# Linear attention and two expert layers on one core: 1 KB runs for the first half block of k, and zero products of a constant

## The chip, the core and the metric

One core of a Trainium2 chip runs the whole program. The metric is device time in microseconds (us): 813.32 us before the change, the median of 3 runs (813.06 to 813.55).

## What is computed

Three layers follow each other, all in float32, on 4 batches of 576 tokens with 8 heads of 64.

```python
q_p, k_p = (phi(q_s), phi(k_s))                # phi: exp(h - max(h)), h = x @ omega.T - |x|^2 / 2
kv = np.einsum('bhsm,bhsd->bhmd', k_p, v)
z = np.sum(k_p, axis=2)
num = np.einsum('bhsm,bhmd->bhsd', q_p, kv)
den = np.einsum('bhsm,bhm->bhs', q_p, z)[..., None] + 1e-06
...
h = x @ w_in
g = np.maximum(h, 0.0) + np.log1p(np.exp(-np.abs(h)))
x = g @ w_out
...
a, b = x @ w1, x @ w2
return ((a * b) @ w3) @ w_out
```

The term |x|^2 / 2 is the same for all features of a token, and so falls out with the maximum that is subtracted.

## The kernel before

The work goes through the k stage (features of k, and their sums with v), the q stage (features of q, the attention's output and its transposes), and then the two expert layers, which are long rows of products. Most products are made three times with operands split into a high and a low part (float32r); the first ones are made in plain f32.

The k stage has eight half blocks i of 512 tokens for four heads each (two half blocks to a batch; the remaining 64 tokens of each batch lie in krest). Half block i is four pieces t of 128 tokens. `load_k(i)` (lines 300 to 307) loads it into one of four buffers rawk. For i > 0 that is one DMA; half block 0 comes as four DMAs, one a piece, so that work can start on the first: pieces 0 and 2 on SyncE's queue (SP), pieces 1 and 3 on ScalarE's (ACT), behind omega (`om`). In DRAM a partition's row of a half block is two pairs of heads with 512 tokens each, so a piece is two runs of 512 B a partition.

`split_k(i)` (lines 309 to 314) makes the high part kt*h on VectorE (DVE) and the low part kt*l. Half block 0 isn't split, but multiplied in f32 (`om`, `rawk`, 8 products in 16 passes). Half block 1 is split in four pieces, the low part on GpSimd (POOL), the others in one piece, the low part on VectorE. `k_feat(i, t)` (lines 362 to 367) multiplies a piece with omega (`project`), takes the maximum of each head on VectorE (`nmax`, line 349), and has ScalarE take the exponentials (`kp`, line 354, four of 128x128 a piece). `kv_sum(i)` multiplies them with v (`vt`) and with the rest (`vrest`, `kpr`), half an array at a time.

TensorE (PE) makes three zero products at the very start, before any data is there. They read a small tile, `edge_t`, that GpSimd has to set to zero first:

```python
warm = ps()
for _ in range(WARM):
    matmul(warm[:, 0:256], edge_t[:, 0:1].to_broadcast([128, 128]), edge_t[:, 0:1].to_broadcast([128, 256]), True, True)
```

The queues are in order: an engine's instructions wait for each other, and so do SyncE's DMAs. The order on each engine is not the order of the code. A scheduler lays it out when the program is built, by its own estimates of durations, so an edit in one place can move instructions elsewhere. The preparation of the first weights (`Job`, lines 138 to 191: `ends` on ScalarE, `upper`, `lower`, the sums and the low parts on VectorE) is mixed into the k and q stages in this way, and so are the casts of q (`qt`).

Of the kernel before, what the change touches and what calls it, by code (L numbers as in the profile page):

```python
# [19 lines left out]
F32 = mybir.dt.float32  # L20
FR = mybir.dt.float32r
# [6 lines left out]
B, H, S, D = 4, 8, 576, 64  # L28
# [4 lines left out]
KT = 4  # L33
# [12 lines left out]
KBUF = 3  # L46
# [13 lines left out]
FOLD_RATE = 2.2  # L60
LAST_RATE = 1.2
KEEP = 4
WARM = 3
WO_AHEAD = 3
GAP = 3
FILL = [18, 19, 20]
# [5 lines left out]
def body(ctx: ExitStack, tc: tile.TileContext, q, k, k_rest, v, v_rest, om_t, w_in, w_out, w12, w3, wo, out):  # L72
    nc = tc.nc
# [9 lines left out]
    def ps():  # L83
        return ps_.tile([128, 512], F32, tag="ps", name="ps")
# [10 lines left out]
    def matmul(o, a, b, start, stop, **kw):  # L95
        nc.tensor.matmul(out=o, lhsT=a, rhs=b, start=start, stop=stop, **kw)  # L96

    def mm3(o, ahi, alo, bhi, blo, first, last, **kw):
        matmul(o, ahi, bhi, first, False, **kw)
        matmul(o, ahi, blo, False, False, **kw)  # L100
        matmul(o, alo, bhi, False, last, **kw)

    ident = cp.tile([128, 128], F32, name="ident")
# [161 lines left out]
    edge_t = edge.tile([128, 24], F32, name="edge")  # L265
# [3 lines left out]
    K_ = kstack.enter_context(tc.tile_pool(name="K_", bufs=1, side="right"))  # L269
# [4 lines left out]
    def pair(name, bufs):  # L274
        n = small.get(name, (None, 1))[1]
        if n:
            small[name] = sm.tile([128, 2, 4], F32, tag=name, bufs=bufs, name=name), 0
        else:
            small[name] = small[name][0], 1
        return small[name][0][:, 1 - bool(n)]  # L280
# [9 lines left out]
    kt, vt, kps, kpr, kvs, qts, kacc, raw = {}, {}, {}, {}, {}, {}, {}, {}  # L290
# [5 lines left out]
    def split(hi, lo, f, low=None):  # L296
        nc.vector.tensor_copy(out=hi, in_=f)
        (low or nc.gpsimd).tensor_tensor(out=lo, in0=f, in1=hi.bitcast(F32), op=ALU.subtract)

    def load_k(i):  # L300
        if i < 2 * B:
            raw[i] = K_.tile([128, 2, 512], F32, tag="rawk", bufs=4, name="rawk")
            if i:
                nc.sync.dma_start(out=raw[i], in_=k[i])
            else:
                for t in range(KT):
                    (nc.scalar if t % 2 else nc.sync).dma_start(out=raw[i][:, :, 128 * t:128 * t + 128], in_=k[i][:, :, 128 * t:128 * t + 128])

    def split_k(i):
        if 0 < i < 2 * B:  # L310
            kt[i] = kt[i - KBUF] if i > KBUF else [K_.tile([128, 2, 512], FR, name=f"kt{i}{x}") for x in "hl"]
            n = 128 if i == 1 else 512
            for o in range(0, 512, n):
                split(*[x[:, :, o:o + n] for x in (*kt[i], raw[i])], nc.gpsimd if i == 1 else nc.vector)

    def load_v(i):
        if i < 2 * B:
# [21 lines left out]
    def project(lhs):  # L339
        pj = ps()  # L340
        for p in range(2):
            a = lhs(p)
            if len(a) == 2:
                mm3(pj[:, 256 * p:256 * p + 256], *a, *om_s, True, True)
            else:
                matmul(pj[:, 256 * p:256 * p + 256], *a, om, True, True)
        pj = pj.rearrange("p (h m) -> p h m", h=4)
        nmax = pair("nmax", 4)
        nc.vector.tensor_reduce(out=nmax, in_=pj, axis=AX.X, op=ALU.max, negate=True)  # L349
        return pj, nmax  # L350

    def features(pj, nmax, dst):
        for h in range(4):
            nc.scalar.activation(out=dst[:, h, :], in_=pj[:, h, :], func=AF.Exp, bias=nmax[:, h:h + 1])  # L354
# [3 lines left out]
    def flush(n):  # L358
        while len(waiting) > n:
            waiting.pop(0)()  # L360

    def k_feat(i, t):
        if t == 0:
            kps[i] = K_.tile([128, KT, 4, M], F32, tag="kp", bufs=3, name="kp")
        p = project(lambda p: [x[:, p, 128 * t:128 * t + 128] for x in kt.get(i, [raw[0]])])
        waiting.append(lambda: features(*p, kps[i][:, t]))
        flush(0)

# [325 lines left out]

    nc.scalar.dma_start(out=om, in_=om_t)
    load_k(0)
    nc.scalar.preload_act_table_set("exp_and_others")
    warm = ps()
    for _ in range(WARM):
        matmul(warm[:, 0:256], edge_t[:, 0:1].to_broadcast([128, 128]), edge_t[:, 0:1].to_broadcast([128, 256]), True, True)  # L700
    make_identity(nc, ident)
    nc.vector.tensor_scalar(out=om, in0=om, scalar1=float(D) ** -0.25, scalar2=None, op0=ALU.mult)
    split(*om_s, om)
# [9 lines left out]

    load_krest(0)
    load_k(1)
    split_k(1)
    load_v(0)
    load_vrest(0)
    load_k(2)
    split_k(2)  # L720
    load_v(1)
    load_k(3)
# [76 lines left out]
    for s in range(NW):  # L799
        n = min(WB, NF * 512 - WB * s)  # L800
# [351 lines left out]
def _layout(i):  # L1152
    import numpy as np

    def words(a):
        return np.ascontiguousarray(a).view(np.int64)

    q = i["q"].transpose(1, 3, 0, 2).reshape(4, 128, NT // 128, 128).transpose(2, 1, 0, 3)
    k = i["k"].transpose(0, 1, 3, 2).reshape(B, 2, 2, 128, S)
    k_main = k[..., :512].reshape(2 * B, 2, 128, 512).transpose(0, 2, 1, 3)  # L1160
    k_rest = k[..., 512:].reshape(B // 2, 2, 2, 2, 128, 64).transpose(4, 0, 2, 3, 1, 5).reshape(128, B, 2, 128)
    v = np.ones((B, 2, S, 4, D + 1), i["v"].dtype)
    v[..., :D] = i["v"].reshape(B, 2, 4, S, D).transpose(0, 1, 3, 2, 4)
    v_main = v[:, :, :512].reshape(2 * B, KT, 128, 4, D + 1).transpose(0, 2, 1, 3, 4)
    v_rest = v[:, :, 512:].reshape(B // 2, 2, 2, 64, 4, D + 1).transpose(1, 3, 0, 2, 4, 5).reshape(128, B, 4, D + 1)

    om = np.zeros((128, 2 * M), i["omega"].dtype)
    om[:D, :M] = om[D:, M:] = i["omega"].T

    def rows(w, n):  # L1170
        return w.reshape(-1, n, 128, w.shape[1]).transpose(0, 2, 1, 3).reshape(-1, 128, n * w.shape[1])

    def blocks(w, n):
        r, c = w.shape
        return w.reshape(r // 128, 128, c // 128 // n, n, 128).transpose(2, 1, 3, 0, 4).reshape(c // 128 // n, 128, -1)

    def quads(w):

        x = w.reshape(2, 2, 128, -1, 2, 128).transpose(3, 2, 0, 4, 1, 5)
        x = np.stack([x[:, :, 0, 0], x[:, :, 0, 1], x[:, :, 1, 1], x[:, :, 1, 0]], axis=2)  # L1180
        return x.reshape(x.shape[0], 128, 1024)

    w12 = np.stack([i["moe2_w1"].reshape(DM, NJ, 128), i["moe2_w2"].reshape(DM, NJ, 128)], axis=2).reshape(DM, -1)
    return {
        "q": np.ascontiguousarray(q),
        "k": np.ascontiguousarray(k_main),
        "k_rest": np.ascontiguousarray(k_rest),
        "v": np.ascontiguousarray(v_main),
        "v_rest": np.ascontiguousarray(v_rest),
        "om": om,  # L1190
        "w_in": words(quads(i["moe_w_in"])),
        "w_out": words(rows(i["moe_w_out"], NF)[0]),
        "w12": words(quads(w12)),
        "w3": words(blocks(np.ascontiguousarray(i["moe2_w3"].T), 1)),
        "wo": words(rows(i["moe2_w_out"], 1)),
    }
# [19 lines left out]
```

## Time and profile before

| what | value |
|---|---|
| median of 3 runs | 813.32 us (813.06 to 813.55) |
| the profiled execution's own time | 814.26 us |
| its span, first to last instruction | 812.1 us |
| TensorE busy (PE), 5462 products | 805.6 us, 99% |
| weight loads busy (PEld) | 752.9 us, 93% |
| VectorE busy (DVE) | 599.9 us, 74% |
| ScalarE busy (ACT) | 442.0 us, 54% |
| GpSimd busy (POOL) | 25.8 us, 3% |
| moved by DMA | 150.04 MB, 185 GB/s in the mean |

Shares are means over stages with different limits; a stage is to be read by itself. A product's record begins when it enters the array and its end is modelled, so products overlap in the records, and their spacing tells the pace. An f32 product stands as two records. A row of a timeline gives the start in us, the time that the merged records cover, the engine, the line, what is written from what, and in brackets how long the engine was idle before, and what ended that.

### The profile page before, as it was taken

The page shows a single profiled execution, that of the slowest core. Times are in us where ns is not written, and L with a number is a line of the kernel's source. Part 1 is how long each engine was busy: PE and PEld are TensorE (multiplying, and loading weights), DVE is VectorE, ACT ScalarE, POOL GpSimd, SP SyncE. Part 2 cuts the span into 40 slices and gives each one's busy share as a digit, 9 for nine tenths or more (in the row PEclk, how much of TensorE's full clock was granted, in tenths as well). Part 3 has the DMA queues.
Part 4 walks back from the last instruction along what each step waited for, and adds up shares of the span by engine and source line. Part 5 has one row for each costly group of instructions (what it writes and reads, how often), then busy time and mean ns, then how long its engine had stood idle before and what let it go on. Part 6 is the DMA issues. An engine that isn't in the chain of part 4 may idle for free.

```text
span 812.1 us, 14425 instructions
## 1 busy us (share of the span) xinstructions
PE 805.6 (99%) x5462; PEld 752.9 (93%) x5462; DVE 599.9 (74%) x1019; ACT 442.0 (54%) x862; POOL 25.8 (3%) x29
## 2 busy tenths in 40 slices
PE   9999999999999999999999999999999999999998
PEld 8989999999999998888888889999999998889998
DVE  6899899878755676755469733898988776889951
ACT  6899998557445676745456522422434223674430
POOL 3033300000000000000000000000000000000000
PEclk9999999999999999999999999999999999999999
DMA  9833535665545558687994632365565556353212
GB/s 279 339 97 107 175 98 165 208 207 216 198 148 195 184 191 264 209 262 293 320 308 149 221 117 76 147 217 182 172 217 210 188 176 235 116 171 130 78 49 79
DMA packets 75861, 150.04 MB, mean 185 GB/s; under 512 B 7184, under 2 KB 44688, under 8 KB 75792
## 3 DMA queue, kind: packets, MB, share of 16 engines
q1 hardware_dynamic: 64016, 101.55, 37.6%
q10 hardware_dynamic: 11776, 47.57, 17.3%
q8 instruction: 43, 0.70, 0.4%
q14 instruction: 26, 0.21, 0.1%
HBM read 98.24 MB, written 50.86 MB: 184 GB/s over the span
## 4 chain that ended last, share of the span: by engine, by line
PE 92%; ACT 4%; DVE 3%; DMA 1%; issue 1%; POOL 0%; DVEq 0%; ACTq 0%; POOLq 0%
PE ps L96 89%; PE ps L409 2%; ACT kp L354 2%; PE ps L439 1%; DMA xq<-xd 1%; ACT qp L354 1%; DVE s L462 0%; DVE c L517 0%; DVE nmax L349 0%; ACT f L138 0%; ACT raw L139 0%; DVE u L517 0%; DVE f L142 0%; DVE f L148 0%; ACT kv L389 0%
## 5 line engine op out<-in xcount | busy, mean ns | idle before, releaser
L96 PE MATMUL ps<-dhi,lo 128*128 128x512 f32 x256 | 99.6, 389 | 0.0
L96 PE MATMUL ps<-dlo,hi 128*128 128x512 f32 x256 | 99.6, 389 | 0.0
L96 PE MATMUL ps<-dhi,hi 128*128 128x512 f32 x256 | 99.4, 389 | 0.0
L517 DVE TENSOR_TENSOR c<-ps,u 128x384 f32<-128x384 f32 x144 | 71.5, 549 | 0.9
L642 DVE TENSOR_TENSOR dlo<-dn,dhi 128x512 fp32r<-128x512 f32 x64 | 43.8, 689 | 38.3 <-ACT dhi L641 23.7
L517 DVE TENSOR_TENSOR u<-ps,p 128x384 f32<-128x384 f32 x48 | 26.7, 556 | 56.3 <-PE ps L96 54.6
L138 ACT ACTIVATE f<-raw,bias 128x1024 f32<-128x1024 int16 (+2 forms) x43 | 46.5, 1089 | 35.6 <-DMA raw<-in_w 9.7
L641 ACT CAST dhi<-dn 128x512 fp32r<-128x512 f32 x64 | 39.3, 617 | 44.6 <-DVE dlo L642 26.6
L142 DVE SCALAR_TENSOR_TENSOR f<-raw,f 128x1024 int32<-128x1024 f32 (+2 forms) x43 | 45.1, 1049 | 23.3 <-ACT raw L139 22.7
L557 ACT ACTIVATE c<-c 128x384 f32<-128x384 f32 x72 | 35.0, 524 | 45.7 <-DVE c L517 42.2
L524 ACT COPY p<-ps 128x384 f32<-128x384 f32 x48 | 23.0, 480 | 63.3 <-PE ps L96 45.9
L96 PEld LDWEIGHTS ps<-dhi,lo 128*128 128x128 f32 x256 | 48.0, 188 | 10.1
L96 PEld LDWEIGHTS ps<-dlo,hi 128*128 128x128 f32 x256 | 48.0, 188 | 10.0
L96 PEld LDWEIGHTS ps<-dhi,hi 128*128 128x128 f32 x256 | 48.0, 188 | 9.8
L349 DVE TENSOR_REDUCE nmax<-ps 128x4 f32<-128x512 f32 x72 | 46.6, 682 | 6.1 <-PE ps L96 5.4
L139 ACT ACTIVATE raw<-raw,bias 128x1024 f32<-128x1024 int16 (+2 forms) x43 | 46.4, 1083 | 0.5
L148 DVE SCALAR_TENSOR_TENSOR f<-raw,f 128x1024 int32<-128x1024 int32 (+2 forms) x43 | 45.0, 1046 | 0.5
L354 ACT ACTIVATE qp<-ps,nmax 128x128 f32<-128x128 f32 x144 | 44.3, 542 | 1.1 <-DVE nmax L349 1.1
L354 ACT ACTIVATE kp<-ps,nmax 128x128 f32<-128x128 f32 x128 | 35.6, 485 | 7.4 <-DVE nmax L349 7.2
L96 PE MATMUL ps<-xs1h,thi 128*128 128x384 f32 x96 | 32.3, 336 | 0.2 <-DVE c L517 0.2
L96 PE MATMUL ps<-xs2h,thi 128*128 128x384 f32 x96 | 32.3, 336 | 0.0
L96 PE MATMUL ps<-xs2l,thi 128*128 128x384 f32 x96 | 32.3, 336 | 0.0
(257 smaller groups left out, 2342.3 us busy)
## 6 DMA issues: line engine op xcount, KB each, us to landing
dn<-gd SPq DMA_DIRECT2D x64, 256.0 KB, 4.2
raw<-in_w ACTq DMA_DIRECT2D x16, 1023.8 KB, 5.8
gd<-c SPq DMA_DIRECT2D x80, 192.0 KB, 3.5
pd<-c SPq DMA_DIRECT2D x48, 192.0 KB, 2.3
raw<-in_w_out ACTq DMA_DIRECT2D x10, 767.8 KB, 4.8
raw<-in_w_in ACTq DMA_DIRECT2D x6, 1023.8 KB, 5.2
rawq<-in_q SPq DMA_DIRECT2D x18, 256.0 KB, 2.9
xd<-xs SPq DMA_DIRECT2D x18, 256.0 KB, 2.9
```

The lines of the kernel that those rows point to most:

```text
L96: nc.tensor.matmul(out=o, lhsT=a, rhs=b, start=start, stop=stop, **kw)
L138: nc.scalar.activation(out=self.f, in_=top, func=AF.Relu, scale=TOP, bias=bias[:, 0:1])
L139: nc.scalar.activation(out=self.words(1, F32, 2), in_=top, func=AF.Identity, scale=TOP, bias=bias[:, 1:2])
L142: nc.vector.scalar_tensor_tensor(out=self.f.bitcast(I32), in0=self.words(1, F32, 2), scalar=-2.0 ** 31, in1=self.f, op0=ALU.max, op1=ALU.min)
L148: nc.vector.scalar_tensor_tensor(out=fi, in0=self.words(0, I32, 2), scalar=13, in1=fi, op0=ALU.logical_shift_right, op1=ALU.bitwise_or,)
L349: nc.vector.tensor_reduce(out=nmax, in_=pj, axis=AX.X, op=ALU.max, negate=True)
L354: nc.scalar.activation(out=dst[:, h, :], in_=pj[:, h, :], func=AF.Exp, bias=nmax[:, h:h + 1])
L517: nc.vector.tensor_tensor(out=z, in0=bank, in1=y, op=ALU.add)
L524: nc.scalar.copy(out=p6, in_=b1)
L557: nc.scalar.activation(out=dst, in_=src, func=AF.Softplus)
L641: nc.scalar.copy(out=hi, in_=got[m])
L642: nc.vector.tensor_tensor(out=lo, in0=got.pop(m), in1=hi.bitcast(F32), op=ALU.subtract)
```

## The change

The zero products become five of 128 columns instead of three of 256, and they read a column of zeros that the framework sets up itself, ahead of the barrier at which the engines start. The layout of k puts the four pieces of a half block one behind the other, so that a piece is one run of 1 KB a partition; the tiles rawk and kt* follow it. Piece 3 of half block 0 moves from ScalarE's queue to SyncE's.

```diff
-WARM = 3
+WARM = 5
...
-            raw[i] = K_.tile([128, 2, 512], F32, tag="rawk", bufs=4, name="rawk")
+            raw[i] = K_.tile([128, KT, 2, 128], F32, tag="rawk", bufs=4, name="rawk")
...
-                    (nc.scalar if t % 2 else nc.sync).dma_start(out=raw[i][:, :, 128 * t:128 * t + 128], in_=k[i][:, :, 128 * t:128 * t + 128])
+                    (nc.scalar if t == 1 else nc.sync).dma_start(out=raw[i][:, t], in_=k[i][:, t])
...
-            kt[i] = kt[i - KBUF] if i > KBUF else [K_.tile([128, 2, 512], FR, name=f"kt{i}{x}") for x in "hl"]
-            n = 128 if i == 1 else 512
-            for o in range(0, 512, n):
-                split(*[x[:, :, o:o + n] for x in (*kt[i], raw[i])], nc.gpsimd if i == 1 else nc.vector)
+            kt[i] = kt[i - KBUF] if i > KBUF else [K_.tile([128, KT, 2, 128], FR, name=f"kt{i}{x}") for x in "hl"]
+            n = 1 if i == 1 else KT
+            for t in range(0, KT, n):
+                split(*[x[:, t:t + n] for x in (*kt[i], raw[i])], nc.gpsimd if i == 1 else nc.vector)
...
-        p = project(lambda p: [x[:, p, 128 * t:128 * t + 128] for x in kt.get(i, [raw[0]])])
+        p = project(lambda p: [x[:, t, p, :] for x in kt.get(i, [raw[0]])])
...
+    zeros = nc.const_aps.tensor_like(0.0, ident)
     for _ in range(WARM):
-        matmul(warm[:, 0:256], edge_t[:, 0:1].to_broadcast([128, 128]), edge_t[:, 0:1].to_broadcast([128, 256]), True, True)
+        matmul(warm[:, 0:128], zeros, zeros, True, True)
...
-    k_main = k[..., :512].reshape(2 * B, 2, 128, 512).transpose(0, 2, 1, 3)
+    k_main = k[..., :512].reshape(2 * B, 2, 128, KT, 128).transpose(0, 2, 3, 1, 4)
```

With the tiles, the order of the instructions changes in the k stage and the first half of the q stage; behind that each engine has the same order as before. Three places of it follow.

The start of SyncE's queue, before and then changed (rawk from in_k at L307 are pieces of half block 0, at L304 whole half blocks):

```order
L307 DMA rawk<-in_k 128x2x128 x2
L708 DMA krest<-in_k_rest 128x512
L304 DMA rawk<-in_k 128x1024
L319 DMA vt<-in_v 128x1040
L712 DMA vrest<-in_v_rest 64x1040
```

```order
L307 DMA rawk<-in_k 128x256 x3
L709 DMA krest<-in_k_rest 128x512
L304 DMA rawk<-in_k 128x1024
L319 DMA vt<-in_v 128x1040
L713 DMA vrest<-in_v_rest 64x1040
```

Three pieces stand ahead of everything else instead of two.

VectorE from the second piece of half block 0 on, before and then changed (kt1, kt2 and kt3 are the buffers of half blocks 1, 2 and 3, h and l the high and low parts; nmax is the maximum of one piece):

```order
L349 TENSOR_REDUCE nmax<-ps 128x4 x2
L297 CAST kt1h<-rawk 128x2x128 x4
L349 TENSOR_REDUCE nmax<-ps 128x4 x5
L297 CAST kt2h<-rawk 128x1024
L349 TENSOR_REDUCE nmax<-ps 128x4
L298 TENSOR_TENSOR kt2l<-rawk,kt2h 128x1024
L349 TENSOR_REDUCE nmax<-ps 128x4 x2
L297 CAST kt3h<-rawk 128x1024
```

```order
L349 TENSOR_REDUCE nmax<-ps 128x4 x2
L297 CAST kt1h<-rawk 128x256 x4
L349 TENSOR_REDUCE nmax<-ps 128x4 x6
L297 CAST kt2h<-rawk 128x1024
L349 TENSOR_REDUCE nmax<-ps 128x4
L298 TENSOR_TENSOR kt2l<-rawk,kt2h 128x1024
L349 TENSOR_REDUCE nmax<-ps 128x4
L297 CAST kt3h<-rawk 128x1024
```

One reduction has moved from behind the split of half block 2 to the place ahead of it.

VectorE when the buffers kt1 to kt3 are filled for the second time, half blocks 4 to 6, before and then changed:

```order
L297 CAST kt1h<-rawk 128x1024
L298 TENSOR_TENSOR kt1l<-rawk,kt1h 128x1024
L297 CAST kt2h<-rawk 128x1024
L349 TENSOR_REDUCE nmax<-ps 128x4
L298 TENSOR_TENSOR kt2l<-rawk,kt2h 128x1024
L349 TENSOR_REDUCE nmax<-ps 128x4 x3
L297 CAST kt3h<-rawk 128x1024
L298 TENSOR_TENSOR kt3l<-rawk,kt3h 128x1024
L349 TENSOR_REDUCE nmax<-ps 128x4 x4
```

```order
L297 CAST kt1h<-rawk 128x1024
L298 TENSOR_TENSOR kt1l<-rawk,kt1h 128x1024
L349 TENSOR_REDUCE nmax<-ps 128x4
L297 CAST kt2h<-rawk 128x1024
L349 TENSOR_REDUCE nmax<-ps 128x4
L298 TENSOR_TENSOR kt2l<-rawk,kt2h 128x1024
L349 TENSOR_REDUCE nmax<-ps 128x4 x2
L297 CAST kt3h<-rawk 128x1024
L349 TENSOR_REDUCE nmax<-ps 128x4
L298 TENSOR_TENSOR kt3l<-rawk,kt3h 128x1024
```

One reduction stands ahead of the cast of kt2h that stood behind it, and one more between the two steps of kt3.

## Rows read from the trace of the kernel before

**Rows 1.** Busy by stretch: PE, PEld, DVE, ACT, POOL (count); clock, DMA share, GB/s.

```profile
10.00:60.00 50.00, 48.80 (x851) 45.65 (x850) 46.02 (x66) 46.58 (x160) 9.39 (x9) 1.00 0.71 244
60.00:125.00 65.00, 64.39 (x892) 59.87 (x891) 59.46 (x158) 63.49 (x187) 12.87 (x10) 1.00 0.41 123
125.00:812.00 687.00, 683.35 (x3695) 640.39 (x3693) 490.98 (x788) 328.36 (x509) 0.00 (x0) 1.00 0.55 186
```

**Rows 2.** Timeline of TensorE's products and weight loads in the first 4 us.

```profile
0.92 2.93 PE L96 MATMUL ps<-edge 128*128 128x256 f32 x6 [0.92 <-POOL edge L266]
3.64 0.63 PE L96 MATMUL ps<-om,rawk 128*128 128x256 f32 x1
...
0.91 2.21 PEld L96 LDWEIGHTS ps<-edge 128*128 128x128 f32 x6 [0.91 <-POOL edge L266]
```

**Rows 3.** Timeline of the other engines and of the DMA issues, first 3.5 us.

```profile
0.24 0.10 POOL L1204 MEMSET const-float32-0.0<- 128x1 f32 x1 [0.24 <-issue]
...
0.81 0.09 DVE L259 MEMSET bias<- 128x1 f32 x2 [0.81 <-PEq L1204]
2.84 0.29 DVE L702 TENSOR_SCALAR om<-om 128x256 f32<-128x256 f32 x1 [1.94 <-DMA om<-in_om]
...
0.75 1.32 SPq L307 DMA_DIRECT2D rawk<-in_k  x2
...
0.74 0.39 ACTq L695 DMA_DIRECT2D om<-in_om  x1
```

**Rows 4.** DMA issues from 0.7 to 1 us: KB each, us from issue to landing.

```profile
om<-in_om ACTq DMA_DIRECT2D x1, 128.0 KB, 2.1
rawk<-in_k SPq DMA_DIRECT2D x1, 128.0 KB, 2.6
```

**Rows 5.** DMA queues: q10 (ACT) in 1.7:2.2, q1 (SP) in 2.5:2.75; packets, MB, share.

```profile
q10 hardware_dynamic: 85, 0.08, 48.5%
...
q1 hardware_dynamic: 141, 0.07, 93.4%
```

**Rows 6.** Timeline of TensorE from 4 to 8 us, products and weight loads.

```profile
4.06 1.49 PE L96 MATMUL ps<-om,rawk 128*128 128x256 f32 x3
6.17 0.81 PE L96 MATMUL ps<-om,rawk 128*128 128x256 f32 x3
...
5.57 2.52 PEld L96 LDWEIGHTS ps<-om,rawk 128*128 128x128 f32 x12 [0.74 <-DMA rawk<-in_k]
```

**Rows 7.** Timeline of VectorE from 8 to 16 us, and the product that uses kt2l first.

```profile
8.58 1.99 DVE L297 CAST kt1h<-rawk 128x256 fp32r<-128x256 f32 x4 [1.08 <-DMA rawk<-in_k]
10.49 3.07 DVE L349 TENSOR_REDUCE nmax<-ps 128x4 f32<-128x512 f32 x5
14.68 1.21 DVE L298 TENSOR_TENSOR kt2l<-rawk,kt2h 128x1024 fp32r<-128x1024 f32 x1
...
16.05 0.28 PE L96 MATMUL ps<-omh,kt2l 128*128 128x256 f32 x1
```

**Rows 8.** Timeline of VectorE and of ScalarE from 24 to 31 us.

```profile
24.34 0.69 DVE L297 CAST kt2h<-rawk 128x1024 fp32r<-128x1024 f32 x1
24.94 0.68 DVE L349 TENSOR_REDUCE nmax<-ps 128x4 f32<-128x512 f32 x1
...
25.66 1.14 ACT L354 ACTIVATE kp<-ps,nmax 128x128 f32<-128x128 f32 x4 [1.40 <-DVE nmax L349]
27.39 3.21 ACT L354 ACTIVATE kp<-ps,nmax 128x128 f32<-128x128 f32 x12 [0.59 <-DVE nmax L349]
31.05 1.14 ACT L354 ACTIVATE kp<-ps,nmax 128x128 f32<-128x128 f32 x4 [0.17 <-DVE nmax L349]
```

**Rows 9.** Timeline of TensorE from 48 to 63 us, where it waited for ScalarE.

```profile
49.89 0.34 PE L96 MATMUL ps<-vt,kp 128*64 128x65 f32 x4 [0.44 <-ACT kp L354]
...
58.19 1.88 PE L409 MATMUL ps<-ident,qp 128*128 128x128 f32 x7 [0.28 <-ACT qp L354]
...
62.29 0.84 PE L409 MATMUL ps<-ident,qp 128*128 128x128 f32 x3 [0.36 <-ACT qp L354]
```

## The prediction

> **What bounds the kernel now.** I read the busy times by stretch first. TensorE is busy for 48.8 of the 50 us from 10 to 60, 64.4 of 65 from there to 125, and 683.4 of 687 after that; ScalarE (the fourth pair) has 46.6 of 50 and 63.5 of 65 in the first two and 328 of 687 in the last [rows 1]. So after 125 us only TensorE counts, and the change leaves the order of the instructions there as it was: what it does before 125 us arrives at the end whole, neither more nor less. Before 125 us TensorE and ScalarE run nearly abreast, and a wait of either is worth something only if the other isn't late as well.
>
> Next I read the timeline of the first microseconds. TensorE starts at 0.92, when POOL has written edge, and its three zero products (six records, since each of these f32 products stands as two passes) fill it until the first real product at 3.64 [rows 2]. That product needs omega, which lands at 0.74 + 2.1 = 2.84 and is scaled by 3.13, and piece 0 of k, which lands at 0.75 + 2.6 = 3.35 [rows 3, 4]. Passes are then 0.43 us apart (three of them take 1.49: two spacings and one length of 0.63); after a wait of the weight loads for piece 1, at 5.57, they are 0.216 apart (three take 0.81) [rows 6]. That is the lower and the upper of TensorE's two levels, 1.2 and 2.4 GHz, told by the spacing, as the granted clock is recorded as 1.00 throughout; the rise lies between 5.57 and 6.17.
>
> Last I read who waits in the k stage. VectorE stands idle for 1.08 us until half block 1 lands, and from 8.58 it has no gap up to the low part of half block 2 [rows 7]. ScalarE waits three times for a reduction, 1.40, 0.59 and 0.17 us [rows 8], and TensorE later waits three times for ScalarE, 0.44, 0.28 and 0.36 us [rows 9].
>
> **The change part by part.** *The zero products.* Six passes took (3.64 - 0.92) / 6 = 0.45 us each [rows 2]. Ten passes over half the columns are 10 x 0.227 = 2.27 us. They read a constant that POOL wrote at 0.24, so they start with the first instruction behind the opening barrier, where VectorE's stands at 0.81 [rows 3]: the end is at 3.08. The upper bound goes by the weight loads, six in 2.21 us [rows 2]: ten would take 3.7 and end at 4.5, costing up to 0.9 at the lower level. I take 3.08, because in [rows 2] the products follow each other by their columns and the loads run beside them. TensorE then idles a little, as it waits for data.
>
> *The pieces of half block 0.* Each is now 128 runs of 1 KB, the form of omega's load, which took 0.39 us to issue and 2.1 to land; a piece took 0.66 to issue (two in 1.32) and 2.6 to land [rows 3, 4]. So piece 0 lands between 2.85 and 3.35, and the first real product starts between 3.42 and 3.64; I take 3.49, a gain of 0.15 (0 to 0.22, against the bound above). Piece 1 stays second on ScalarE's queue, behind omega. It came so late that after four passes, which end at 3.64 + 4 x 0.43 = 5.35, TensorE stood until 5.57, a loss of 0.22 [rows 2, 6]. It is now needed at 5.2; between its old time (no gain) and 1.17 + 2.1 = 3.3, I take it as in time, since omega alone stands ahead of it in its queue and what moves beside it is shorter: gain 0.22. Both gains, 0.37 us, lie in time at the lower level. They are 0.37 / 0.43 = 0.86 passes, and what is saved behind the rise is 0.86 x 0.216 = **0.2 us** (0 to 0.37).
>
> *The other queues.* A record of 512 B takes 0.934 x 16 x 250 / 141 = 26.5 ns of a DMA engine, one of 1 KB 0.485 x 16 x 500 / 85 = 45.6 ns [rows 5]. Half block 0 is 1024 of the first or 512 of the second: 1.70 or 1.46 us of sixteen engines, 0.24 less. SyncE issues three pieces instead of two, but in 3 x 0.39 = 1.17 instead of 1.32 us, 0.15 less; what stands behind them (the rest of k, half block 1, v) moves up by both, 0.39 us. ScalarE issues one piece less and loads its table sooner; I cost that at nothing, as its next work behind the table waits for the first piece's product and maximum, which end after 5 us.
>
> The Trainium skill ("DMA: Bandwidth & Descriptors", Specifications) gives 512 B as the least transfer for full line rate, so by it the longer runs would save nothing. The trace disagrees: 26.5 ns for half of what takes 45.6. By the rule the 0.39 would be 0.15 and the forecast below 0.24 us later.
>
> *VectorE at 10 us.* The order puts six reductions, not five, between the casts of half block 1 and the cast of half block 2. One is 3.07 / 5 = 0.61 us [rows 7]. The low part of half block 2 ended at 14.68 + 1.21 = 15.89, and TensorE used it at 16.05. Now it ends at 15.89 + 0.61 - 0.39 = 16.11 and would be used at 16.05 - 0.2 = 15.85: a new wait of 0.26 (0 to 0.81, by how much sooner half block 1 lands). So the start's gain is **spent by 16 us: +0.06 us**. Queued behind the low part are the remaining reductions, which are one fewer.
>
> *VectorE at 24 us.* The order puts a reduction ahead of the cast of the next half block, which takes 24.94 - 24.34 = 0.60 us [rows 8]. ScalarE's four exponentials behind that reduction start 0.60 sooner. ScalarE has next to no idle time after 31 us [rows 1], so this lead is kept until TensorE waits for it: the three waits of [rows 9] sum to 1.08 us and can take it up. I count **-0.60 us**. The lower bound of the gain is 0, if another order costs it again; the upper is all three waits of [rows 8], 2.16 us. The job of win[0] moves back on ScalarE and VectorE by a few rows; I cost it at nothing, as TensorE asks for win[0] only in the q stage, more than 30 us later.
>
> Sum: +0.06 - 0.60 = -0.54 us. Against the profiled execution of 814.26 us that is 813.72; that execution lies 0.94 above the median of 813.32, which I take as the base: **812.8 us**. A measurement can tell about 0.2%, 1.63 us, from no change.
>
> **The rivals.** *More of ScalarE's idle time goes.* The reordered reductions may leave none of the 2.16 us, and half block 1 may land early enough that nothing waits at 16 us: -0.2 - 2.16 = -2.36, 811.0 us. For it: reductions move ahead of two casts or subtractions in that stretch, not one. Against it: TensorE's waits for ScalarE, the place where a lead is cashed, sum to 1.08 us in [rows 9].
>
> *The order buys nothing.* The lead is lost to the rows that move back on ScalarE: +0.06, 813.4 us.
>
> *The clock rises later (slower).* The zero products end at 3.08 instead of running into the first real one, and each has half the columns. If TensorE's rise waits for activity without that gap, passes that now stand 0.216 apart stay at 0.43. Each costs 0.214; the twelve passes of pieces 1 to 3 cost 2.6, and 813.32 - 0.54 + 2.6 = 815.4 us. It decides from 1.63 + 0.54 = 2.17 us on, eleven passes. Against it: TensorE also stood still from 5.35 to 5.57, just ahead of the first pass that was followed quickly [rows 6]. The Trainium skill ("TensorE: Matmul & The Clock Gate", Part 1) says that the throttled level is the default and that activity releases it, and it speaks of gaps as what undoes this; that agrees with the slow start here, and no row shows what a gap at this place does.
>
> **How the numbers follow.** I give my forecast 0.58, with a range of its own from 812.2 to 813.4; more idle time gone 0.20; nothing bought 0.16; the late clock 0.06. The first and third are within 0.2%: 0.74; faster 0.20, slower 0.06. The range reaches from 811.2, most of the way to the first rival, to 813.9, which holds a wait of 0.81 at 16 us with nothing bought (813.32 - 0.2 + 0.81).
>
> **What would show it.** Right: zero products from about 0.8 to 3.1; the first weight load of a real product by 3.3; no wait before piece 1; sixth reduction, and the low part of half block 2 at about 16.1 with TensorE waiting 0.2 to 0.3 us there; ScalarE's 1.40 us wait down to about 0.8; the waits near 49.9, 58 and 62 us smaller by 0.6 together; all stages after 125 us of equal length. Wrong: passes still 0.43 apart behind 6.2 us; piece 1 still landing after 5; a total more than 0.5 us away from where the stage up to 125 us puts it.

## The result

| | before | changed |
|---|---|---|
| median | 813.36 us, 6 runs (813.06 to 813.77) | 817.86 us, 6 runs (816.66 to 819.12) |
| the profiled execution's own time | 814.26 us | 819.12 us |
| its span | 812.1 us | 817.0 us |

The changed kernel takes 1.0056 times as long, with an interval of 1.0043 to 1.0069. That is 4.5 us **slower**, where 812.8 us and a range from 811.2 to 813.9 were forecast. The profiled execution of the changed kernel was the longest of its six, 1.3 us over the median, so the places of the loss are read from it and the sizes are judged by medians.

**Where the time went.** The busy time by stretch of the changed kernel, with the columns of [rows 1]:

```profile
10.00:60.00 50.00, 49.24 (x854) 46.57 (x852) 44.02 (x67) 44.90 (x154) 9.00 (x9) 1.00 0.69 237
60.00:125.00 65.00, 61.66 (x810) 56.15 (x810) 57.66 (x149) 60.17 (x181) 14.98 (x11) 1.00 0.38 112
125.00:817.00 692.00, 688.21 (x3783) 645.34 (x3781) 495.88 (x799) 333.38 (x523) 0.00 (x0) 1.00 0.55 186
```

TensorE is busy for 61.66 us between 60 and 125 us, where [rows 1] show 64.39. ScalarE, the fourth pair, is busy for less in both of the first stretches: 44.90 for 46.58, and 60.17 for 63.49. In the long last stretch TensorE is busy for 99.5% of the time, as before.

A finer reading comes from setting the start of one product against that of the same product in the kernel before (the same place in TensorE's order, counted from the first product that reads k). Differences in us:

| product of the kernel before at | changed kernel later by |
|---|---|
| 3.64, first real product | 0.81 |
| 10.42, first of half block 1 | 2.17 |
| 21.21, a product of the sums with v | 1.47 |
| 49.89 | 1.54 |
| 62.89, first half of the q stage | 1.81 |
| 75.27 | 3.85 |
| 87.77 | 3.98 |
| 108.12 | 5.18 |
| 625.13 | 4.67 |
| 808.34, the last | 4.67 |

So this execution has two losses, one by 10 us, of which 1.8 us are still there at 62.89, and one between 63 and 108 us. Behind 108 us nothing more is lost.

**The start.** Timeline of the changed kernel, first 12 us:

```profile
0.74 0.42 ACTq L695 DMA_DIRECT2D om<-in_om  x1
...
0.78 2.48 PE L96 MATMUL ps<-const-float32-0.0 128*128 128x128 f32 x10 [0.78 <-PEq L1205]
...
4.10 0.29 DVE L703 TENSOR_SCALAR om<-om 128x256 f32<-128x256 f32 x1 [3.20 <-DMA om<-in_om]
...
4.45 6.22 PE L96 MATMUL ps<-om,rawk 128*128 128x256 f32 x16 [1.19 <-DVE om L703]
...
10.10 1.99 DVE L297 CAST kt1h<-rawk 128x256 fp32r<-128x256 f32 x4 [1.14 <-DMA rawk<-in_k]
```

The zero products run from 0.78 to 3.26, ten passes as forecast. But omega, issued at 0.74, lands only at 4.08: VectorE waits for it until 4.10, where [rows 3] show 2.84, and TensorE stands idle for 1.19 us. From 4.45 on there is no wait between the pieces, yet the sixteen passes take 6.22 us, and pairs of them closer than 0.3 us come first at 9.64, where the kernel before has them from 5.96 on ([rows 6] show the next ones, from 6.17): TensorE stays at 1.2 GHz some 3.7 us longer, told by the spacing. Piece 0 of k is late too, at 3.89 instead of 3.31.

**Near 37 us.** The chain of waits of the changed kernel from 20 to 45 us (start, duration, what):

```profile
20.00 9.01 PE ps L96 x192
29.00 0.23 SPq L319
29.23 0.05 issue
29.29 8.01 DMA raw<-in_w_in
37.29 0.02 issue
37.32 1.25 ACT f L138
```

`raw<-in_w_in` is the load of win[0], the first weights that are prepared beside the k and q stages. It is issued at 29.29, behind a load of v (`SPq L319`) that TensorE holds up until it has read the buffer. ScalarE is ready for it at 35.93. The timeline of ScalarE from 24 to 38 us shows three waits, where [rows 8] show three others:

```profile
28.29 2.17 ACT L354 ACTIVATE kp<-ps,nmax 128x128 f32<-128x128 f32 x8 [0.47 <-DVE nmax L349]
32.46 1.92 ACT L354 ACTIVATE kp<-ps,nmax 128x128 f32<-128x128 f32 x7 [0.59 <-DVE nmax L349]
...
37.32 1.25 ACT L138 ACTIVATE f<-raw,bias 128x1024 f32<-128x1024 int16 x1 [1.39 <-DMA raw<-in_w_in]
```

ScalarE's waits for reductions have gone from 2.16 to 1.06 us, the way the forecast had it and further. A new one of 1.39 us, for the load, takes their place. In the kernel before, SyncE's queue from 22 to 28 us reads:

```profile
22.78 0.42 SPq L130 DMA_DIRECT2D raw<-in_w_in  x1
27.48 0.33 SPq L319 DMA_DIRECT2D vt<-in_v  x1
```

There the load stands ahead of that load of v. It is issued 6.5 us earlier, and ScalarE never waits for it.

**Near 73 us.** The timeline of VectorE in the changed kernel from 36 to 75 us, casts of q and what they wait for (L142 is an addition in win[0]'s preparation):

```profile
37.99 0.43 DVE L297 CAST qt<-rawq 128x512 fp32r<-128x512 f32 x1 [1.62 <-DMA rawq<-in_q]
...
59.57 1.23 DVE L142 SCALAR_TENSOR_TENSOR f<-raw,f 128x1024 int32<-128x1024 f32 x1 [2.12 <-ACT raw L139]
60.71 0.42 DVE L297 CAST qt<-rawq 128x512 fp32r<-128x512 f32 x1
...
67.59 0.41 DVE L297 CAST qt<-rawq 128x512 fp32r<-128x512 f32 x1
...
71.12 0.15 DVE L426 TENSOR_SCALAR den<-ps 128x4 f32<-128x4 f32 x1
73.65 0.43 DVE L297 CAST qth<-rawq 128x512 fp32r<-128x512 f32 x1 [2.38 <-DMA rawq<-in_q]
```

And in the kernel before, from 52 to 71 us:

```profile
55.84 0.42 DVE L297 CAST qt<-rawq 128x512 fp32r<-128x512 f32 x1
57.92 1.23 DVE L142 SCALAR_TENSOR_TENSOR f<-raw,f 128x1024 int32<-128x1024 f32 x1 [1.66 <-ACT raw L139]
...
64.65 0.43 DVE L297 CAST qt<-rawq 128x512 fp32r<-128x512 f32 x1
...
69.22 1.10 DVE L297 CAST qth<-rawq 128x512 fp32r<-128x512 f32 x1
```

The fifth cast stood ahead of L142 at 55.84; now it stands behind it and behind L142's wait, at 60.71. The later casts are late with it (67.59 for 64.65). q has five load buffers, and SyncE can load into one when GpSimd has read its low part out of it. So the load for qth is issued at 69.44 instead of 66.51 and lands at 73.63 instead of 69.03. Of these 4.6 us, 2.9 come from the issue; the rest is the load itself, which took 4.2 us where it had taken 2.5. VectorE, which takes its instructions in order, waits 2.38 us for it. The chain of waits from 60 to 82 us shows what is queued behind:

```profile
69.44 4.18 DMA rawq<-in_q
73.63 0.02 issue
73.65 0.43 DVE qth L297
74.08 0.09 DVE den L427
...
78.97 0.10 DVE den L427
79.06 0.05 issue
79.11 2.03 PE ps L96 x38
```

`den` is the attention's denominator. TensorE's timeline has the price:

```profile
74.84 1.15 PE L96 MATMUL ps<-kv,qpt 128*64 128x65 f32 x32 [0.86 <-DVE den L427]
...
79.11 0.36 PE L96 MATMUL ps<-omh,qt 128*128 128x256 f32 x1 [0.96 <-DVE den L427]
```

Neither wait exists in the kernel before. The Trainium skill ("Perfetto Trace Analysis", Tensor Engine Instruction) calls VectorE, ScalarE and GpSimd strict first in, first out; the trace agrees for VectorE, as what the reciprocal of `den` reads was written by 71.27 (the row of 71.12), and the reciprocal starts at 73.99, behind the cast that waited.

**What the change did to the lists.** Both late loads come from the order in which the scheduler lays out the instructions. SyncE's queue, around its twentieth DMA, before and changed:

```
L304 DMA rawk<-in_k 128x1024
L130 DMA raw<-in_w_in 128x4095
L319 DMA vt<-in_v 128x1040
L325 DMA rawq<-in_q 128x512 x2
```

```
L304 DMA rawk<-in_k 128x1024
L319 DMA vt<-in_v 128x1040
L130 DMA raw<-in_w_in 128x4095
L325 DMA rawq<-in_q 128x512
L319 DMA vt<-in_v 128x1040
```

The kernels with parts of the change tell which one does this, by the order in their traces. It isn't the tiles, as "The change" has it. With the new layout alone, and pieces 1 and 3 on ScalarE's queue, the order is that of before. With the new zero products, alone or with the layout, one row of VectorE differs: a reduction stands ahead of the cast of kt2h at 24 us, the very one that the prediction priced at -0.60 us. With piece 3 moved to SyncE's queue, alone or with the layout, the order is that of the changed kernel but for a few rows (one early cast of q, one reduction beside kt3l, one load of q).

### The profile page after: what moved, and what is told of

Same layout as the page of the kernel before. It is cut to its first block, busy times and chain, and to the rows that moved or that the text cites. A ratio compares the mean times of both kernels' runs of the same rounds, so it can differ in the third digit from the quotient of the medians.

```text
span 817.0 us, 14427 instructions
## 1 busy us (share of the span) xinstructions
PE 807.1 (99%) x5466; PEld 754.8 (92%) x5466; DVE 599.6 (73%) x1019; ACT 441.9 (54%) x862; POOL 26.4 (3%) x29
## 4 chain that ended last, share of the span: by engine, by line
PE 92%; ACT 3%; DMA 2%; DVE 1%; issue 1%; SPq 0%; ACTq 0%; DVEq 0%
PE ps L96 90%; PE ps L409 2%; ACT kp L354 1%; PE ps L439 1%; DMA raw<-in_w_in 1%; ACT qp L354 1%; DMA rawq<-in_q 1%; DMA om<-in_om 0%; ACT f L138 0%; ACT raw L139 0%; ACT kpr L354 0%; DVE nmax L349 0%; DVE tlo L191 0%; DVE xt L430 0%; ACT qpt L411 0%
## 5 line engine op out<-in xcount | busy, mean ns | idle before, releaser
L96 PE MATMUL ps<-dhi,hi 128*128 128x512 f32 x256 | 99.5, 389 | 0.0
L142 DVE SCALAR_TENSOR_TENSOR f<-raw,f 128x1024 int32<-128x1024 f32 (+2 forms) x43 | 45.1, 1049 | 19.3 <-ACT raw L139 19.0
L179 DVE TENSOR_TENSOR lo<-f,hi 128x512 fp32r<-128x512 f32 (+2 forms) x43 | 29.4, 705 | 4.2 <-ACT hi L174 4.1
```

The source lines that it names most:

```text
L142: nc.vector.scalar_tensor_tensor(out=self.f.bitcast(I32), in0=self.words(1, F32, 2), scalar=-2.0 ** 31, in1=self.f, op0=ALU.max, op1=ALU.min)
L179: nc.vector.tensor_tensor(out=self.lo[:, a:b], in0=self.f[:, a:b], in1=self.hi[:, a:b].bitcast(F32), op=ALU.subtract)
```

## The experiments

The first four runs ask which part of the change makes the loss, and their expectations name the theories as they stood then. In the later ones two stand against each other. **O**: the order of the instructions makes the loss. From there on it is split: **Ow**, win[0]'s load and what hangs on it; **Oq**, the late casts of q; **Ok**, the reductions of the k stage. **S**: the late start does it (omega, half block 1, the clock). Medians in us; ratios are to the kernel before on the same chip, whose medians were 813.55 for the first four runs, 813.7 for the next four, and 813.65 for the last three.

| run | median (lowest to highest, runs) | ratio, interval |
|---|---|---|
| zero products only | 814.12 (812.57 to 816.69, 12) | 1.0005 [0.9995, 1.0015] |
| layout only | 814.01 (812.74 to 815.39, 12) | 1.0004 [0.9994, 1.0013] |
| piece 3 moved only | 818.11 (814.62 to 818.97, 11) | 1.0044 [1.0032, 1.0056] |
| all but the move | 814.92 (812.92 to 815.93, 12) | 1.0010 [0.9999, 1.0022] |
| whole change, ten zero products | 814.57 (812.79 to 816.71, 10) | 1.0014 [1.0001, 1.0026] |
| layout and move, old zero products | 816.66 (814.50 to 820.09, 10) | 1.0031 [1.0016, 1.0047] |
| whole change, one cast of q up | 816.45 (815.17 to 819.62, 10) | 1.0039 [1.0025, 1.0053] |
| whole change, all casts of q up | 816.25 (815.14 to 817.04, 10) | 1.0033 [1.0023, 1.0043] |
| whole change, win[0]'s load up | 814.34 (813.60 to 815.71, 11) | 1.0009 [0.9997, 1.0021] |
| the same with the old zero products | 813.84 (812.84 to 814.70, 12) | 1.0002 [0.9993, 1.0011] |
| kernel before, win[0]'s load down | 816.29 (815.12 to 817.86, 7) | 1.0035 [1.0023, 1.0047] |

And how late a product was against the profile of the kernel before, by its time there. A profile is one execution, and more than a microsecond in the first columns can be chance: the kernel of the last row has its instructions in the order of before up to 22 us, and is still 1.75 us late at 21.21:

| run | 10.42 | 21.21 | 49.89 | 62.89 | 75.27 | 108.12 | last |
|---|---|---|---|---|---|---|---|
| changed kernel | 2.17 | 1.47 | 1.54 | 1.81 | 3.85 | 5.18 | 4.67 |
| zero products only | 1.98 | 1.14 | 0.49 | 0.05 | 0.05 | 0.17 | -0.27 |
| piece 3 moved only | 1.07 | 1.49 | 1.75 | 1.85 | 3.14 | 3.43 | 2.94 |
| layout and move | 0.05 | -0.69 | -1.32 | -1.32 | -0.23 | -0.01 | 0.00 |
| one cast up | 1.78 | 0.94 | 1.12 | 1.44 | 1.50 | 1.78 | 2.31 |
| win[0]'s load up | 1.32 | 1.06 | 1.27 | 1.06 | 0.96 | 0.27 | -0.18 |
| before, load down | 0.87 | 1.75 | 1.16 | 0.91 | 1.71 | 2.00 | 2.00 |

### Each part alone

The zero products:

```diff
-WARM = 3
+WARM = 5
+    zeros = nc.const_aps.tensor_like(0.0, ident)
-        matmul(warm[:, 0:256], edge_t[:, 0:1].to_broadcast([128, 128]), edge_t[:, 0:1].to_broadcast([128, 256]), True, True)
+        matmul(warm[:, 0:128], zeros, zeros, True, True)
```

> The new zero products alone; layout, queues and VectorE's order are those of before. Theory O (the order of VectorE and SyncE in the q stage costs about 3 us, the late start about 1.5): nothing of the q stage is lost, so at most the gap between zero products and first real product costs, 813.4 to 815; passes 0.43 us apart last longer only if the gap holds TensorE's clock down. Theory S (everything follows from the start): if the gap holds the clock down, 815 to 818 with the waits near 74 and 79 us as in the changed kernel.

Measured: 814.12 us. This run has the changed kernel's late clock without its late omega. The timeline of its TensorE, first 11 us:

```profile
0.78 2.47 PE L96 MATMUL ps<-const-float32-0.0 128*128 128x128 f32 x10 [0.78 <-PEq L1205]
3.64 6.83 PE L96 MATMUL ps<-om,rawk 128*128 128x256 f32 x16 [0.39 <-DMA rawk<-in_k]
```

The first real product comes at 3.64 as before, and still the sixteen passes take 6.83 us; passes closer than 0.3 us come first at 9.88. At 10 us the run is 1.98 us late. By 62.89 it is 0.05 late. So a late start can be **absorbed** in the k stage: ScalarE waits less for reductions there, 1.1 us for 2.2 between 20 and 63 us. Part of that may be the one reduction that stands elsewhere in this kernel, against what was expected of its order:

```profile
24.12 0.69 DVE L349 TENSOR_REDUCE nmax<-ps 128x4 f32<-128x512 f32 x1
24.73 0.68 DVE L297 CAST kt2h<-rawk 128x1024 fp32r<-128x1024 f32 x1
```

In [rows 8] the cast stands first. Twelve runs can't tell the total from the kernel before; the interval reaches 0.15%, 1.2 us.

The layout, with pieces 1 and 3 on ScalarE's queue and the old zero products (the diff of the change, without these two edits):

> The 1 KB runs alone, pieces on the queues as before, old zero products; the order on every engine is that of before. Theory O: within 0.5 us of before, 813 to 814. Theory L (the 1 KB packets of k hold omega up, so that it lands at 4 instead of 2.8 us): omega lands after 3.5 us and the time is 814.5 to 816.

Measured: 814.01 us, no difference. Here the clock rises at 6.25, and omega lands at 3.58.

The move:

```diff
-                    (nc.scalar if t % 2 else nc.sync).dma_start(out=raw[i][:, :, 128 * t:128 * t + 128], in_=k[i][:, :, 128 * t:128 * t + 128])
+                    (nc.scalar if t == 1 else nc.sync).dma_start(out=raw[i][:, :, 128 * t:128 * t + 128], in_=k[i][:, :, 128 * t:128 * t + 128])
```

> Piece 3 on SyncE's queue alone, 512 B runs, old zero products; this alone gives the order of the changed kernel on VectorE, ScalarE and SyncE. Theory O: 815.5 to 817, with TensorE waiting near 72 to 80 us behind a cast of q on VectorE that waits for its load. Theory S: within 0.5 us of before.

Measured: 818.11 us, as slow as the whole change. Omega lands at 2.88 and the clock rises at 6.14, so nothing of the late start is left in it but half block 1, which lands at 10.07. VectorE waits 1.6 us for the load of qth, and the product of 75.27 is 3.14 late. The load of win[0] is issued at 29.30 and lands at 36.34, late as in the changed kernel, but ScalarE is then still busy, and doesn't wait for it:

```profile
36.68 1.37 ACT L138 ACTIVATE f<-raw,bias 128x1024 f32<-128x1024 int16 x1
```

So a run can be as slow as the changed kernel without ScalarE's wait of 1.39 us; what the two share, besides half block 1, is the late load, the late cast (60.75) and the wait for qth's load.

The change without the move:

```diff
-                    (nc.scalar if t == 1 else nc.sync).dma_start(out=raw[i][:, t], in_=k[i][:, t])
+                    (nc.scalar if t % 2 else nc.sync).dma_start(out=raw[i][:, t], in_=k[i][:, t])
```

> The whole change but for piece 3, which stays on ScalarE's queue; order of before. Theory O: the start's cost alone, 814 to 815.5. Theory S: as slow as the changed kernel, 817 to 818.

Measured: 814.92 us; at most 0.2% slower than before. Most of the loss is in the one edit of a queue's name. That edit changes both which queue carries a piece and the lists; the next runs tell these apart.

### The queue or the lists

Ten zero products in the whole change (`WARM = 10`). Piece 3 stays on SyncE's queue, but the scheduler then happens to lay out q's loads and casts, and win[0]'s load, as before.

> The whole change, with ten zero products where it has five. Piece 3 stays on SyncE's queue, but with ten the scheduler lists the instructions nearly as in the kernel before (VectorE's list differs by one reduction, ScalarE's by the issue of piece 3, and q's loads and casts stand where they stood). The zero products should end near 5.1 us and close the gap ahead of the first real product, which starts later than in the changed kernel by 0.6. Theory O (the loss is made by the order of the instructions, not by the queue): between 813 and 815.5 us, and no wait of VectorE for a load of q above 1 us between 63 and 80 us. Rival S (the loss is made by the late start: late omega, late half block 1, late rise of the clock): 817 us or more, as omega and half block 1 land as late as in the changed kernel and the products start later still. A clock that rises by 7 us would say that the gap of idle time had delayed it; one that rises after 9 us would say that the gap is not what does it.

Measured: 814.57 us; S wanted 817 or more. The late start is the worst of all: the first real product stands at 5.18, and the product of 21.21 is 2.33 us late. The timeline of its TensorE:

```profile
0.79 4.61 PE L96 MATMUL ps<-const-float32-0.0 128*128 128x128 f32 x20 [0.79 <-PEq L1205]
5.18 3.83 PE L96 MATMUL ps<-om,rawk 128*128 128x256 f32 x16
```

With no gap, and twice the zero products, the sixteen passes take 3.83 us, and those closer than 0.3 us begin at 5.61. By the sign that was set, the gap had delayed the clock; but twice the products is a second difference, so this run doesn't separate the two. VectorE waits 1.04 us for a load of q, just over the bound of 1. The late start isn't absorbed here, with nearly the old lists: the product of 62.89 is 1.27 us late and the last one 2.43. The profiled execution was this run's longest, at 816.71 us, but the interval, 0.1 to 2.1 us slower, leaves out no change as well, and the late start is the likely part of it.

The layout and the move, with the old zero products (the changed kernel's lists):

> The new layout of k and piece 3 on SyncE's queue, with the old three zero products (edge, 256 columns). The order of the instructions is that of the changed kernel. Theory O: 816.5 to 818.5 us, as slow as the changed kernel, although the zero products run up to the first real product and the clock should rise before 7.5 us. Rival S: the start is better than in the changed kernel by what the clock loses there (1.5 to 2 us), so 815 to 816.

Measured: 816.66 us, at the lower end of O's range, and above S's (by the interval, 815.0 to 817.5 us, S's 815 to 816 isn't ruled out). The start is good: 0.05 us late at 10 us, and 1.32 early at 62.89. The q stage takes 1.3 us of it back, with VectorE waiting 1.4 us for the load of qth. Its runs scatter over 5.6 us. The profiled one, 814.50, is the shortest of ten, so its row in the second table looks better than the median.

### Which rows of the lists

One cast of q in the changed kernel:

```diff
-            split(*qt, raw[t])
+            with (tc.high_priority() if t in (4,) else ExitStack()):
+                split(*qt, raw[t])
```

> The whole change; only q's cast of tile 4 gets a high priority. Against the changed kernel it moves up two places on VectorE, ahead of the addition of win[0]'s features that waits for ScalarE, and one later cast goes one place down; all other engines' lists are the same as in the changed kernel. Theory Oq (the loss of the q stage comes from q's casts that stand late, so that a rawq buffer comes free late, a load lands late, and VectorE waits for it with the sums of the denominators queued behind): the cast starts 3 to 5 us earlier (60.7 to about 56), the load that VectorE waited 2.4 us for lands before its cast is due, and the total is 1.5 to 3 us below the changed kernel: 815 to 816.5. Rival Ok (the loss is made by the reductions of the k stage in another order, and the wait in the q stage only stands beside it): less than 0.8 us below the changed kernel, 817 to 818.

Measured: 816.45 us, inside Oq's range. That is 1.41 below the changed kernel, but the two intervals overlap, so the gain is read from the trace more than from the total. VectorE's timeline:

```profile
56.34 0.58 DVE L297 CAST qt<-rawq 128x512 fp32r<-128x512 f32 x1
...
59.19 1.23 DVE L142 SCALAR_TENSOR_TENSOR f<-raw,f 128x1024 int32<-128x1024 f32 x1 [1.67 <-ACT raw L139]
...
70.62 1.11 DVE L297 CAST qth<-rawq 128x512 fp32r<-128x512 f32 x1
```

The cast stands at 56.34, the wait for qth's load is gone, and with it TensorE's two waits for `den`: from 62.89 to 108.12 this kernel loses 0.34 us, where the changed one loses 3.37. Oq is right for this stretch of the profile. ScalarE's wait for win[0]'s load is still there, 1.50 us, and 2.8 us to the kernel before remain.

All casts up (the same context around every `split` of the kind, without the condition):

> The whole change; all of q's casts and their low parts get a high priority. The casts of tiles 1 and 2 move far up on VectorE (from places 61 and 62 to 49 and 51), the later ones up by a few places; the k stage's order up to there is that of the changed kernel. Theory Oq: if the loads keep ahead of the casts, at least as good as with one cast moved, 814 to 816.5; if the early casts wait for loads that have not landed, that wait is new and stands near 45 to 50 us. Rival Ok: 817 to 818, as the k stage is unchanged.

Measured: 816.25 us, inside Oq's range at its upper end. The two casts that moved far up (now at 40.88 and 42.35) don't wait for their loads; the first cast of q waits 1.93 us at 37.66, as it did in the changed kernel (1.62). But ScalarE's waits for reductions grow to 4.4 us between 20 and 63 us, from 1.1, and TensorE is 4.09 us late at 49.89. It gets 1.5 us of that back in the q stage. Moving everything up gains no more than moving one.

The load of win[0] in the changed kernel:

```diff
-            (self.queue or nc.scalar).dma_start(out=self.raw[:, :4 * self.n - 1], in_=self.src.bitcast(I16)[:, 1:])
+            with (tc.high_priority(30) if self is win[0] else ExitStack()):
+                (self.queue or nc.scalar).dma_start(out=self.raw[:, :4 * self.n - 1], in_=self.src.bitcast(I16)[:, 1:])
```

> The whole change; only the load of win[0] gets an earlier priority. On SyncE's queue it moves one place up, ahead of a load of v that waits for TensorE to free its buffer, which is where it stands in the kernel before; q's casts, which hang on win[0]'s work, then stand on VectorE nearly as in the kernel before, too. The k stage's reductions, the late omega and the late rise of the clock stay those of the changed kernel. Theory Ow (the loss is made by win[0]'s load behind the load of v and by what follows from it: ScalarE's wait for that load near 37 us and q's late casts): the load is issued before 26 us and lands by 35, ScalarE does not wait for it, VectorE waits for a load of q by less than 1.2 us near 73 us, and the total is 813.5 to 815.5 us. Rival Ok (reductions of the k stage): 816.5 to 818. Rival S (late start): 816 to 818.

Measured: 814.34 us, 3.52 below the changed kernel, and not to be told from the kernel before. SyncE's queue from 24 to 29 us, and then ScalarE's timeline:

```profile
24.80 0.42 SPq L131 DMA_DIRECT2D raw<-in_w_in  x1
28.55 0.33 SPq L320 DMA_DIRECT2D vt<-in_v  x1
```

```profile
33.88 1.29 ACT L139 ACTIVATE f<-raw,bias 128x1024 f32<-128x1024 int16 x1
```

(Lines are one higher here.) The load goes out ahead of the load of v again and lands at 31.89, and ScalarE starts on it without a wait. VectorE waits 0.18 us for qth's load instead of 2.38. VectorE's first 44 instructions, up to 36 us, keep the changed kernel's order, the reductions that the prediction spoke of among them, so Ok falls. The late start is in it too: 1.32 us late at 10 us, and the clock rises at 8.35. In this profile it is made good by 151 us, so S falls as what makes most of the loss; the interval, up to 0.21%, leaves it a share.

The same with the old zero products:

> As the run before, with the old three zero products. Theory Ow, with the late start absorbed by ScalarE's idle time in the k stage: within 0.8 us of the run before, between 813 and 815 us. Rival S: 1 to 2 us below the run before.

Measured: 813.84 us, 0.5 below the run before; the intervals overlap. VectorE waits 1.43 us for qth's load here too, and TensorE 0.5 us for `den`, so that wait by itself doesn't make a slow run. In the three pairs of runs on one chip, the five short zero products (with the row that moves with them) go with the higher median: by 0.57 us alone, 0.91 with the layout, 0.50 here. No pair is clear of noise, and none shows that they are free.

The kernel before, with no part of the change, and win[0]'s load down:

```diff
-            (self.queue or nc.scalar).dma_start(out=self.raw[:, :4 * self.n - 1], in_=self.src.bitcast(I16)[:, 1:])
+            with (tc.high_priority(-200) if self is win[0] else ExitStack()):
+                (self.queue or nc.scalar).dma_start(out=self.raw[:, :4 * self.n - 1], in_=self.src.bitcast(I16)[:, 1:])
```

> The kernel before, with its own layout, pieces and zero products; only the load of win[0] gets a later priority. On SyncE's queue it then stands two places down, behind the load of v that waits for TensorE and behind a load of q, and the lists of VectorE, ScalarE and SyncE from there on are nearly those of the changed kernel. The start must be that of the kernel before. Theory Ow: the load is issued near 28 us and lands after 34, ScalarE waits for it, and the total is 816 to 818.5 us, the loss without any part of the change. Rivals S and Ok: 813 to 814.5, since the start and the k stage's first 25 us are untouched.

Measured: 816.29 us, 2.6 slower than the kernel before, and clear of noise. The chain of waits from 25 to 45 us is that of the changed kernel:

```profile
29.34 0.23 SPq L320
29.57 0.05 issue
29.62 6.92 DMA raw<-in_w_in
36.54 0.02 issue
36.56 1.24 ACT f L139
```

ScalarE waits 0.59 us for the load and VectorE 1.15 us for that of qth. So 2.6 of the 4.5 us are there without any of the change's edits, and with VectorE's first 41 instructions in the order of before, where S and Ok wanted 813 to 814.5. One expectation failed: the start isn't that of the kernel before. Half block 1 lands at 9.88, not 8.55, though all its loads are the same; that scatters between executions (see the end).

## Why the prediction was wrong

Against the changed kernel, each taken by itself: one cast of q up gives back 1.4 us, within the scatter; win[0]'s load up gives back 3.5 (it moves q's casts as well); and the old zero products on top of that 0.5 more, within the scatter.

- **The step that failed** is "The job of win[0] moves back on ScalarE and VectorE by a few rows; I cost it at nothing, as TensorE asks for win[0] only in the q stage". TensorE isn't who asks. ScalarE does, at 35.9 us in the changed kernel, and on VectorE win[0]'s addition L142 holds up what is queued behind it. The step also left out win[0]'s DMA, on SyncE's queue, where one place cost 6.5 us of issue time, because the load that it went behind was waiting for TensorE. q's loads and casts weren't priced at all. In its place the runs showed: moving that one load back up leaves 814.34 us, and moving it down in the kernel before costs 2.6.
- **The sum** of +0.06 and -0.60 became +4.5. With the reduction ahead of the cast at 24 us, ScalarE's waits for reductions between 20 and 63 us were 1.06 us in the changed kernel and 1.1 and 1.2 in the two runs that have it and the old lists otherwise, for 2.16 before; but with win[0]'s load up they were 3.1, and 1.7 with the old zero products. The lead wasn't cashed where the prediction had it: TensorE's three waits of [rows 9], 1.08 us, are 0.27, 0.43 and 0.35 in the changed kernel, 1.05. And no total shows it: the run with nearly all of the changed kernel's reductions, win[0]'s load up and the old zero products has 813.84 against 813.65.
- **The zero products** end at 3.26 by the record, the last starts at 2.83, and 3.08 was forecast: about right.
- **The first real product**, forecast at 3.49 (0 to 0.22 us gained, 0.9 lost at most), came at 4.45. The working let piece 0 set it and took omega's landing from the kernel before. Omega landed at 4.08 instead of 2.82, and piece 0 at 3.89, not between 2.85 and 3.35.
- **No wait ahead of piece 1**: right. The gain of 0.2 us was not, since the clock was still at its lower level.
- **The rival of the late clock** was given 0.06, with 815.4 us. What it described happened: passes that were 0.216 us apart stayed at 0.43. The price, 2.6 us that arrive whole, did not: the run with the zero products alone is 1.98 us late at 10 us and 0.05 at 62.89, and its median is 0.57 us up. That TensorE's lateness at 125 us arrives at the end held: the changed kernel is 5.18 late at 108 us and 4.67 at the end. The Trainium skill ("TensorE: Matmul & The Clock Gate", Part 1) says that the number of products at the lower level changes from run to run, and that the ramp's penalty is under 1% of a typical kernel. The runs fit both: the five other profiles with the five short zero products, of five kernels, have the rise between 7.13 and 9.88 us, and on one chip these products change the median by 0.5 to 0.9 us, 0.11% at most.
- **0.39 us on the other queues**: not to be read from these profiles. Half block 1 landed at 10.07 in the changed kernel, at 10.19 in the run with ten zero products, and between 7.47 and 7.98 in five others with the same layout and queues. The Trainium skill ("DMA: Bandwidth & Descriptors", Specifications) gives 512 B as the least transfer for full line rate, by which longer runs gain nothing. The landings don't decide between it and the prediction's 26.5 and 45.6 ns a record: with the layout alone pieces 1 and 2 came sooner, but omega later by 0.76 us and piece 3 at 7.86 for 6.13; over all profiles the last piece landed between 5.59 and 7.09 us with runs of 512 B and between 5.19 and 7.86 with 1 KB.
- **kt2l**: it ended at 18.01 and was used at 18.06, with no wait of TensorE, which was itself late. The new wait of 0.26 us did not come.

What stays open is the split of the 3.5 us between what hangs on the load in the k stage (ScalarE's wait near 37 us is one part, and the run of the move alone was as slow without it) and the casts of q. No run moved the load and left every cast in place. Open as well is how much of the remaining 1 us or so is the late start, and how much of that start is chance.

## What to carry to other kernels

Where a scheduler lays out the order, an edit to one queue at the start can reorder rows tens of microseconds later, and those rows have to be priced as the edit's own. First look for loads that change places in an in-order queue with a load that waits for a buffer: here one place was worth 6.5 us of issue time. A loss at the start isn't the loss at the end: here 1.98 us at 10 us became 0.05 by 62.89 in one profile and 1.18 became 2.43 by the end in another. Where it was absorbed, ScalarE, which runs nearly abreast with TensorE there, stood idle for less (1.1 us for 2.2). That a new wait on ScalarE spends this slack is argued from the traces; no run separates it.

## What the runs showed of the hardware

- **Omega is late when k's pieces are runs of 1 KB.** It landed at 2.82, 2.88, 2.88 and 3.10 us in the four profiles with runs of 512 B, and at 3.58 to 4.08 in the nine with 1 KB, although its own load is the same and was issued first on its queue, at 0.74. Pieces 1 and 2 came earlier with the new layout: 4.22 and 4.03 in the run of the layout alone, for 5.53 and 5.75. Piece 0 gained nothing (3.38 for 3.31). That the faster pieces take their time from omega would fit, and no run separated it.
- **The rise of TensorE's clock came later with the five short zero products.** With that edit alone it moved from 5.96 to 9.88 us. It came at 5.59 to 6.84 us in six profiles with three products of 256 columns (2.93 us of them), at 7.13 to 9.88 in six with five of 128 (2.48 us), and at 5.61 with ten of 128 (4.61 us). A gap didn't always go with a late rise: with the old zero products TensorE stood idle for 0.33 us ahead of the first real product in the run of layout and move, and the rise came at 5.59. Each is one profile of one kernel.
- **Half block 1 lands at 7.5 to 10.2 us in kernels whose first loads are the same.** That is more than the change was to move it (0.39 us), so a single profile does not tell a gain there.
